# Two PSUM banks shared by the two halves of a convolution and the two sweeps of a second product, with every round in a new order

## The chip, the cores and the metric

The kernel runs on one core of a Trainium2 chip. A core has a matrix engine (PE, with its weight loads shown as PEld), a vector engine (DVE), a scalar engine (ACT), a general engine (POOL) and a queue engine (SP). Each engine works through its own list of instructions in order; semaphores tie the lists together. Matrix products land in PSUM, a memory of eight banks that PE, ACT and DVE can reach. The metric is the device time of one execution in microseconds (us).

## The reference

A causal convolution with seven taps, softmax-normalised per head, and behind it a dense layer with a rational activation:

```
w   = softmax(weight)                                  # 8 heads x 7 taps
xc[b,s,h,:] = sum_k w[h,k] * x[b, s-6+k, h, :]         # 8 x 4096 tokens, 192 features
h   = xc @ w_in                                        # 32768 x 2048
P   = a0 + a1*h + a2*h^2 + a3*h^3
Q   = 1 + |b0|*|h| + |b1|*h^2
out = (P / (Q + 1e-6)) @ w_out                         # 32768 x 192
```

All of it is float32. The convolved `xc`, the hidden `h` and the activation never leave the core.

## The kernel before

The 32768 tokens are cut into 64 **chunks** of 512 (`NCH`). The 2048 hidden features are cut into 8 **units** of 256 for each chunk. A chunk passes through three stages.

- **Convolution** (`conv_part`, L301): PE multiplies band matrices of taps. Half 0 (features of the first 128 rows, 36 matmuls) and half 1 (the other 64 rows, for both halves of the tokens, 18 matmuls) each fill one PSUM bank. A float32 matmul leaves two records in the trace, so the halves show as 72 and 36. ACT copies half 0 out, rounded (`xh`, L310), and DVE takes the remainder (`xl`, L319); half 1 is copied by two pieces on ACT (L313) and two on DVE (L324).
- **First product and activation** of a unit (`gemm1`, L336, 10 matmuls into a two-bank tile `hp`, of which there are two). ACT makes `hs` (a copy, L381), `A` (L401) and `B` (L404); POOL makes `t` in two steps, `p` (L387) and `u` (L394), and starts a DMA that adds `B` to `A` (`Q`, L407); DVE finishes the numerator, `v` (L398); ACT takes logarithm and exponential for the reciprocal, `L` (L410) and `Y` (L413, into a PSUM tile of which there is one); DVE makes `m`, `e`, `g` (L417, L422, L426). The last of `hs`, `A`, `B`, `v` of a unit lets PE write the first product of the unit after next into the same `hp`.
- **Second product** (`gemm2`, L353): for one chunk two **sweeps**, `g20` to `g23` for tokens 0 to 255 and `g24` to `g27` for tokens 256 to 511. Each sweep has 16 **quarters** (a to d) of two matmuls, four records each, and sums in one bank over all 16 blocks of features. `out_evac` (L360, ACT) then copies the bank to `ob`, and SP stores it: `O0` for the first sweep, `O1` for the second.

The order is written by hand in three strings: `START` for the first three rounds, `PLAN`, used for each of the rounds 3 to 62, and `END`. A token such as `g13b.1` names a step, its unit, a piece, and how many chunks back it works. In round i PE runs the convolution of chunk i, the first products mostly of chunk i-1 and the second product of chunk i-2. Each engine sees only its own tokens, in the order of the string; `tc.manual_schedule` keeps it for PE, ACT, DVE and POOL.

Two PSUM banks matter for the change. `ps_c` holds one tile, `cps`, and takes both halves of the convolution, one after the other. `ps_o` holds one tile, `op`, and takes both sweeps of the second product, one after the other; only the very last chunk has its first sweep in `ps_c`. The weights are rounded in START, and their steps (`wi..`, `wo..`) use the same two tiles.

Of the kernel before, what the change touches and what calls it, by code (L numbers as in the profile page):

```python
# [39 lines left out]


PLAN = """
c0.0 O1.2 Q1.1 hs2.1 v1.1 Y7.2 p2.1 g20a.1 B2.1 m7.2 g20b.1 u2.1 g13a.1 A2.1 e7.2 L0.1 g13b.1 g7.2 xh0.0
g20c.1 hs3.1 v2.1 g20d.1 Y0.1 g21a.1 p3.1 g21b.1 A3.1 m0.1 g14a.1 Q2.1 B3.1 e0.1 u3.1 g14b.1 L1.1 g0.1
g21c.1 hs4.1 g21d.1 Q3.1 Y1.1 v3.1 g22a.1 g22b.1 B4.1 p4.1 m1.1 g22c.1 A4.1 g15a.1 u4.1 e1.1 L2.1 g15b.1
g1.1 g22d.1 hs5.1 Q4.1 v4.1 g23a.1 Y2.1 g23b.1 p5.1 xl0.0 g23c.1 B5.1 m2.1 g23d.1 u5.1 L3.1 g16a.1 e2.1
O0.1 A5.1 g16b.1 g2.1 Q5.1 g24a.1 hs6.1 v5.1 g24b.1 Y3.1 g24c.1 p6.1 c1.0 A6.1 m3.1 u6.1 g17a.1 L4.1
e3.1 xh1.0 g17b.1 B6.1 g3.1 g24d.1 hs7.1 g25a.1 xl1.0 g25b.1 Y4.1 p7.1 v6.1 g25c.1 A7.1 g25d.1 m4.1 Q6.1
L5.1 g10a.0 u7.1 e4.1 B7.1 g10b.0 g4.1 g26a.1 hs0.0 Q7.1 g26b.1 v7.1 Y5.1 g26c.1 p0.0 g26d.1 B0.0 m5.1
g11a.0 u0.0 A0.0 e5.1 g11b.0 L6.1 g5.1 g27a.1 hs1.0 Q0.0 g27b.1 v0.0 Y6.1 g27c.1 p1.0 g27d.1 L7.1 m6.1  # L50
g12a.0 u1.0 B1.0 e6.1 g12b.0 A1.0 g6.1
"""


# [2 lines left out]


START = """
wia0.0 c0.0 cf0.0 wid0.0 wis0.0 wid1.0 wio0.0 cf1.0 wia1.0 wir0.0 c1.0 wis1.0 xh0.0 wih0.0 wio1.0 xl0.0  # L60
wia2.0 wir1.0 wid2.0 wip0.0 wis2.0 wih1.0 wio2.0 xh1.0 wil0.0 wir2.0 wia3.0 xl1.0 wip1.0 wid3.0 wis3.0
wid4.0 g10a.0 wio3.0 wih2.0 wil1.0 wia4.0 wir3.0 wid5.0 g10b.0 wis4.0 wih3.0 wio4.0 cf2.0 wir4.0 wip2.0
hs0.0 g11a.0 wia5.0 p0.0 wil2.0 A0.0 wis5.0 u0.0 wio5.0 g11b.0 wih4.0 B0.0 wia6.0 wip3.0 hs1.0 wis6.0
Q0.0 wil3.0 wid6.0 p1.0 B1.0 wio6.0 wip4.0 v0.0 wia7.0 wir5.0 A1.0 wis7.0 g12a.0 u1.0 wih5.0 wio7.0
wod0.0 wil4.0 woa0.0 g12b.0 wid7.0 wos0.0 L0.0 woo0.0 Q1.0 v1.0 woa1.0 wir6.0 Y0.0 wos1.0 g13a.0 woo1.0
hs2.0 wir7.0 m0.0 woa2.0 wip5.0 p2.0 wih6.0 e0.0 A2.0 g13b.0 u2.0 g0.0 B2.0 L1.0 wos2.0 wil5.0 hs3.0
Q2.0 v2.0 wip6.0 Y1.0 p3.0 woo2.0 g14a.0 wod1.0 m1.0 B3.0 wor0.0 g14b.0 wod2.0 e1.0 u3.0 wih7.0 woa3.0
wil6.0 A3.0 wos3.0 wip7.0 hs4.0 woo3.0 Q3.0 v3.0 A4.0 p4.0 g1.0 woa4.0 g15a.0 L2.0 wor1.0 wos4.0 Y2.0
woo4.0 g15b.0 u4.0 wil7.0 woa5.0 m2.0 B4.0 c0.1 hs5.0 wos5.0 Q4.0 v4.0 wod3.0 p5.0 L3.0 e2.0 g16a.0
xh0.1 u5.0 B5.0 g2.0 g16b.0 A5.0 xl0.1 Y3.0 woo5.0 Q5.0 c1.1 v5.0 hs6.0 wor3.0 B6.0 m3.0 g17a.0 p6.0  # L70
xh1.1 e3.0 woa6.0 wor2.0 g17b.0 A6.0 wos6.0 u6.0 L4.0 g3.0 hs7.0 woo6.0 xl1.1 Y4.0 Q6.0 v6.0 wod4.0 p7.0
A7.0 m4.0 g10a.1 B7.0 wor4.0 e4.0 g10b.1 woa7.0 u7.0 L5.0 g4.0 hs0.1 wos7.0 Y5.0 p0.1 woo7.0 v7.0 g20a.1
A0.1 Q7.0 g20b.1 L6.0 m5.0 g11a.1 u0.1 wod6.0 e5.0 B0.1 g11b.1 wod5.0 g20c.1 g5.0 hs1.1 Q0.1 g20d.1 v0.1
g21a.1 Y6.0 p1.1 g21b.1 A1.1 m6.0 g12a.1 wor5.0 B1.1 u1.1 e6.0 g12b.1 L7.0 g6.0 g21c.1 hs2.1 c0.2 Q1.1
v1.1 Y7.0 p2.1 g21d.1 A2.1 m7.0 g13a.1 L0.1 u2.1 e7.0 g13b.1 xh0.2 B2.1 g7.0 g22a.1 hs3.1 Q2.1 g22b.1
xl0.2 Y0.1 g22c.1 v2.1 p3.1 c1.2 wod7.0 L1.1 m0.1 g22d.1 wor6.0 g14a.1 xh1.2 u3.1 e0.1 A3.1 g14b.1 g0.1
B3.1 g23a.1 hs4.1 wor7.0 xl1.2 g23b.1 Y1.1 v3.1 Q3.1 g23c.1 g23d.1 B4.1 p4.1 m1.1 g15a.1 L2.1 u4.1 e1.1
g15b.1 O0.1 A4.1 g24a.1 g1.1 hs5.1 g24b.1 Q4.1 v4.1 g24c.1 Y2.1 p5.1 B5.1 m2.1 g16a.1 A5.1 u5.1 e2.1
g16b.1 L3.1 g24d.1 g2.1 hs6.1 g25a.1 Q5.1 v5.1 g25b.1 Y3.1 g25c.1 p6.1 B6.1 m3.1 g17a.1 L4.1 u6.1 e3.1
g17b.1 A6.1 g3.1 g25d.1 hs7.1 g26a.1 Q6.1 v6.1 Y4.1 g26b.1 p7.1 g26c.1 B7.1 m4.1 g10a.2 u7.1 A7.1 e4.1  # L80
g10b.2 L5.1 g4.1 g26d.1 hs0.2 Q7.1 g27a.1 v7.1 Y5.1 g27b.1 p0.2 g27c.1 A0.2 m5.1 g11a.2 u0.2 B0.2 e5.1
g11b.2 L6.1 g5.1 g27d.1 hs1.2 Q0.2 v0.2 Y6.1 p1.2 L7.1 m6.1 g12a.2 u1.2 B1.2 e6.1 g12b.2 A1.2 g6.1
"""


END = """
c0.1 O1.3 Q1.2 hs2.2 v1.2 Y7.3 p2.2 g20a.2 g20b.2 L0.2 m7.3 u2.2 g13a.2 B2.2 e7.3 g13b.2 A2.2 g7.3
g20c.2 Q2.2 hs3.2 g20d.2 v2.2 xh0.1 g21a.2 p3.2 Y0.2 g21b.2 g21c.2 B3.2 u3.2 m0.2 g14a.2 A3.2 e0.2
g14b.2 L1.2 Q3.2 g0.2 g21d.2 hs4.2 g22a.2 v3.2 Y1.2 g22b.2 p4.2 g22c.2 xl0.1 L2.2 g15a.2 u4.2 m1.2 B4.2
g15b.2 e1.2 A4.2 g22d.2 g1.2 hs5.2 c1.1 p5.2 v4.2 g23a.2 xh1.1 g23b.2 Y2.2 Q4.2 g23c.2 L3.2 g23d.2 m2.2  # L90
u5.2 g16a.2 B5.2 e2.2 O0.2 g16b.2 A5.2 g2.2 g24a.2 Q5.2 hs6.2 v5.2 g24b.2 Y3.2 g24c.2 p6.2 xl1.1 g24d.2
L4.2 g17a.2 u6.2 m3.2 B6.2 g17b.2 e3.2 g25a.2 hs7.2 g3.2 g25b.2 A6.2 g25c.2 p7.2 v6.2 g25d.2 Y4.2 g26a.2
u7.2 B7.2 m4.2 g10a.1 A7.2 e4.2 g10b.1 L5.2 Q6.2 g26b.2 g4.2 hs0.1 g26c.2 v7.2 g26d.2 p0.1 Y5.2 g27a.2
B0.1 m5.2 g27b.2 Q7.2 g27c.2 e5.2 u0.1 g27d.2 g11a.1 O1.2 g5.2 A0.1 g20a.1 L6.2 v0.1 Q0.1 g11b.1 Y6.2
g20b.1 hs1.1 m6.2 g20c.1 g12a.1 A1.1 p1.1 e6.2 L7.2 g12b.1 u1.1 g6.2 B1.1 g20d.1 hs2.1 g21a.1 g21b.1
Y7.2 p2.1 v1.1 g21c.1 B2.1 g21d.1 Q1.1 m7.2 g22a.1 A2.1 g13a.1 u2.1 e7.2 L0.1 g13b.1 g7.2 g22b.1 Q2.1
hs3.1 v2.1 g22c.1 Y0.1 g22d.1 p3.1 g23a.1 A3.1 m0.1 g23b.1 u3.1 L1.1 g23c.1 e0.1 g23d.1 B3.1 g14a.1 g0.1
O0.1 Q3.1 g14b.1 v3.1 Y1.1 g20a.0 L2.1 m1.1 g24a.1 B4.1 g24b.1 e1.1 g15a.1 hs4.1 g1.1 A4.1 p4.1 g24c.1
g24d.1 Y2.1 Q4.1 g15b.1 L3.1 m2.1 u4.1 g25a.1 A5.1 g25b.1 e2.1 B5.1 g20b.0 g25c.1 g2.1 hs5.1 g25d.1 v4.1
g26a.1 p5.1 Y3.1 g26b.1 L4.1 m3.1 Q5.1 g26c.1 g26d.1 e3.1 u5.1 g16a.1 g3.1 g27a.1 g16b.1 v5.1 Y4.1  # L100
g27b.1 A6.1 m4.1 g27c.1 B6.1 g27d.1 e4.1 g20c.0 hs6.1 Q6.1 g17a.1 g4.1 O1.1 p6.1 L5.1 g20d.0 Y5.1 g21a.0
u6.1 g17b.1 m5.1 g24a.0 A7.1 e5.1 g21b.0 B7.1 g21c.0 g5.1 g21d.0 hs7.1 Q7.1 g22a.0 v6.1 L6.1 g24b.0 p7.1
g24c.0 Y6.1 g24d.0 u7.1 m6.1 g22b.0 g25a.0 e6.1 g25b.0 g22c.0 g6.1 g25c.0 L7.1 g25d.0 v7.1 Y7.1 g26a.0
g26b.0 m7.1 g22d.0 g26c.0 e7.1 g23a.0 g7.1 g26d.0 g23b.0 g27a.0 g27b.0 g23c.0 g23d.0 g27c.0 O0.0 g27d.0
O1.0
"""


# [5 lines left out]
def kernel(  # L114
# [52 lines left out]
    def load_x(c):  # L167
        t = xs_buf[c % 2]
        nc.sync.dma_start(out=t[0:BLK, 0:3 * XF // 4], in_=xa[c])
        nc.sync.dma_start(out=t[BLK:, 3 * XF // 4:], in_=xb[c])  # L170
# [165 lines left out]
            nc.tensor.matmul(H[k][:, j, :], lhsT=w[:, i, part, j, :], rhs=x, start=(n == 0), stop=(n == len(terms) - 1))  # L336
# [4 lines left out]

    def gemm2(c, u, q):
        pair, r = divmod(u, 4)
        f = 4 * r + q
# [4 lines left out]
        op = O[c, pair]
        g = G[c * UPC + f // 2]  # L350
        for t in range(2):
            tok = (2 * pair + t) * P
            nc.tensor.matmul(op[:, t, 0:D], lhsT=g[:, f % 2, tok:tok + P], rhs=wo_t[:, f, :],  # L353
                             start=(f == 0 and t == 0), stop=(f == FT - 1 and t == 1))
# [60 lines left out]
    def step_m(k):  # L415
        G[k] = gpool.tile([P, 2, CH], F32, name="g")
        nc.vector.scalar_tensor_tensor(out=G[k].rearrange("p a b -> p (a b)"), in0=st[k]["t"], scalar=a0,  # L417
                                       in1=st[k]["y"], op0=ALU.add, op1=ALU.mult)
# [5 lines left out]
    def step_g(k):  # L424
        g = G[k].rearrange("p a b -> p (a b)")
        nc.vector.scalar_tensor_tensor(out=g, in0=st[k]["y"], scalar=2.0, in1=g, op0=ALU.subtract, op1=ALU.mult)  # L426
# [107 lines left out]
```

## Time and profile before

| what | value |
|---|---|
| time, median of 3 runs (range) | 2715.94 us (2715.7 to 2717.48) |
| profiled execution, its own time | 2716.26 us |
| its span, first to last instruction | 2714.5 us |
| busy ACT / DVE / POOL | 94% / 95% / 85% of the span |
| start of the convolution of chunk 3 (first PLAN round) | 119.59 us |
| start of the convolution of chunk 63 (END) | 2615.53 us |
| granted PE clock, mean | 0.997 |

The span is 1.76 us short of the execution's own time. A row of the timeline gives start, duration, engine, line and operands, and in brackets the idle time before it and who ended it; neighbouring rows of one form are merged with a count. The chain of waits inside a window, in order of time, gives the pieces of work that follow each other on the path that ended last: start, length, engine, tile, line and how many instructions. There the end of each piece is the start of the next, so lengths can be added. A row of the windows view gives the stretch and its length, then how long PE, PEld, DVE, ACT and POOL were busy in it (with instruction counts), the granted PE clock, the share of DMA time and GB/s.

### The profile page before, as it was taken

Reading aid. Unit: us, or ns where it says so; the run is one execution under the profiler, and the core shown is the slowest. Engines: PE = TensorE matmul, PEld = TensorE weight load, DVE = VectorE, ACT = ScalarE, POOL = GpSimd, SP = SyncE. Lnnn points to the kernel's source line nnn. Section 1 sums busy time; section 2 is a strip of 40 time slices with the busy share of each in tenths; the row PEclk is TensorE's granted clock in tenths of the full one; section 3 lists DMA queues with packets and bytes.
Section 4 is the critical chain, followed back from the end, with each engine's and each line's share of the span. In section 5 each row is a group of like instructions: output and inputs, shape, how many; then the busy total and the mean of one; then the engine's idle time right before and its main releaser. Section 6 shows DMA issues by size and latency. Waiting matters only on the chain.

```text
span 2714.5 us, 51342 instructions
## 1 busy us (share of the span) xinstructions
PE 2680.2 (99%) x20248; PEld 2414.1 (89%) x20248; DVE 2587.1 (95%) x2293; ACT 2560.7 (94%) x2927; POOL 2302.7 (85%) x1567
## 2 busy tenths in 40 slices
...
GB/s 192 114 123 126 117 123 121 123 124 119 125 122 120 125 121 117 129 119 126 119 122 124 126 117 123 120 123 124 121 125 120 123 124 120 117 129 119 126 102 93
DMA packets 122786, 332.79 MB, mean 123 GB/s; under 512 B 12848, under 2 KB 51888, under 8 KB 122544
## 3 DMA queue, kind: packets, MB, share of 16 engines
...
q10 hardware_dynamic: 432, 0.20, 0.0%
...
## 4 chain that ended last, share of the span: by engine, by line
PE 94%; DVE 2%; POOL 1%; ACT 1%; issue 1%; DMA 0%; ACTq 0%; POOLq 0%; DVEq 0%
PE op L353 47%; PE hp L336 42%; PE cps L301 4%; POOL t L394 1%; DVE t L398 0%; DVE y L422 0%; PE cps L353 0%; POOL t L387 0%; DMA A<-B 0%; ACT y L413 0%; ACT hs L381 0%; DVE g L426 0%; ACT A L401 0%; DMA wb_t<-in_wband 0%; PE cps L278 0%
## 5 line engine op out<-in xcount | busy, mean ns | idle before, releaser
L353 PE MATMUL op<-wo_t,g 128*128 128x192 f32 x8128 | 1411.4, 327 | 0.6 <-DVE wo_t L268 0.6
L353 PEld LDWEIGHTS op<-wo_t,g 128*128 128x128 f32 x8128 | 1341.6, 190 | 41.7 <-POOL t L394 1.3
L394 POOL TENSOR_TENSOR t<-t,hs 128x1024 f32<-128x1024 f32 x512 | 1268.0, 2476 | 31.6
L387 POOL TENSOR_SCALAR t<-hs,cf 128x1024 f32<-128x1024 f32 x512 | 647.5, 1265 | 290.4 <-ACT hs L381 283.2
L336 PE MATMUL hp<-xh,wh_t 128*128 128x512 f32 x2048 | 871.1, 425 | 12.6 <-DVE t L398 12.6
L417 DVE SCALAR_TENSOR_TENSOR g<-t,cf,y 128x1024 f32<-128x1024 f32 x512 | 655.0, 1279 | 80.4 <-ACT y L413 64.6
L398 DVE SCALAR_TENSOR_TENSOR t<-t,cf,hp 128x1024 f32<-128x1024 f32 x512 | 652.1, 1274 | 6.1 <-POOL t L394 2.8
L426 DVE SCALAR_TENSOR_TENSOR g<-y,g 128x1024 f32<-128x1024 f32 x512 | 627.0, 1225 | 17.5
L336 PE MATMUL hp<-xh,wl_t 128*128 128x512 f32 x2048 | 635.7, 391 | 0.0
L381 ACT COPY hs<-hp 128x1024 f32<-128x1024 f32 x512 | 524.5, 1024 | 117.7 <-PE hp L336 104.8
L422 DVE SCALAR_TENSOR_TENSOR y<-A,y 128x1024 f32<-128x1024 f32 x512 | 625.7, 1222 | 0.0
L410 ACT ACTIVATE B<-A 128x1024 f32<-128x1024 f32 x512 | 551.1, 1076 | 4.5 <-DMA A<-B 4.4
L413 ACT ACTIVATE y<-B 128x1024 f32<-128x1024 f32 x512 | 536.8, 1048 | 10.1 <-DVE g L426 4.4
L407 POOL DMA_DIRECT2D A<-B x512 | 480.2, 938 | 66.6 <-ACT A L401 51.6
L401 ACT ACTIVATE A<-hp 128x1024 f32<-128x1024 f32 x512 | 532.9, 1041 | 1.0 <-PE hp L336 0.9
L404 ACT ACTIVATE B<-hp 128x1024 f32<-128x1024 f32 x512 | 529.8, 1035 | 1.5
L336 PEld LDWEIGHTS hp<-xh,wl_t 128*128 128x128 f32 x2048 | 385.3, 188 | 88.9
L336 PEld LDWEIGHTS hp<-xh,wh_t 128*128 128x128 f32 x2048 | 386.3, 189 | 86.8 <-issue 11.5
L336 PE MATMUL hp<-xl,wh_t 128*128 128x512 f32 x1024 | 404.0, 394 | 0.0
L336 PEld LDWEIGHTS hp<-xl,wh_t 128*128 128x128 f32 x1024 | 193.9, 189 | 20.4
L301 PEld LDWEIGHTS cps<-wb_t,xs 128*32 128x32 f32 x6876 | 120.8, 150 | 45.5 <-issue 43.0
L301 PE MATMUL cps<-wb_t,xs 128*32 128x58 f32 x6876 | 137.1, 228 | 9.0 <-DVE cf L230 7.8
...
## 6 DMA issues: line engine op xcount, KB each, us to landing
A<-B POOLq DMA_DIRECT2D x512, 512.0 KB, 4.6
out<-ob SPq DMA_DIRECT2D x128, 192.0 KB, 1.9
...
```

The costliest lines, as they stand in the source:

```text
L336: nc.tensor.matmul(H[k][:, j, :], lhsT=w[:, i, part, j, :], rhs=x, start=(n == 0), stop=(n == len(terms) - 1))
L353: nc.tensor.matmul(op[:, t, 0:D], lhsT=g[:, f % 2, tok:tok + P], rhs=wo_t[:, f, :], start=(f == 0 and t == 0), stop=(f == FT - 1 and t == 1))
L387: nc.gpsimd.tensor_scalar(tile_of(k, "t", work), st[k]["hs"], a3, a2, ALU.mult, ALU.add)
L394: nc.gpsimd.tensor_tensor(out=t, in0=t, in1=st[k]["hs"], op=ALU.mult)
L398: nc.vector.scalar_tensor_tensor(out=t, in0=t, scalar=a1, in1=flat(k), op0=ALU.add, op1=ALU.mult)
L401: nc.scalar.activation(out=tile_of(k, "A", work), in_=flat(k), func=AF.Abs, scale=scales[0])
L404: nc.scalar.activation(out=tile_of(k, "B", work), in_=flat(k), func=AF.Square, scale=scales[1])
L410: nc.scalar.activation(out=st[k]["B"], in_=st[k]["A"], func=AF.Ln, bias=C_Q)
L413: nc.scalar.activation(out=tile_of(k, "y", ps_y), in_=st[k]["B"], func=AF.Exp, scale=-1.0)
L417: nc.vector.scalar_tensor_tensor(out=G[k].rearrange("p a b -> p (a b)"), in0=st[k]["t"], scalar=a0, in1=st[k]["y"], op0=ALU.add, op1=ALU.mult)
L422: nc.vector.scalar_tensor_tensor(out=y, in0=st[k]["A"], scalar=C_Q, in1=y, op0=ALU.add, op1=ALU.mult)
L426: nc.vector.scalar_tensor_tensor(out=g, in0=st[k]["y"], scalar=2.0, in1=g, op0=ALU.subtract, op1=ALU.mult)
```

## The change

The sweeps and the halves are dealt to the banks anew, from chunk 1 on for the sweeps and from chunk 3 on for the halves:

```diff
     def gemm2(c, u, q):
...
-        if f == 0 and c == NCH - 1 and pair == 0:
+        if f == 0 and pair == 0 and c >= 1:
             O[c, pair] = ps_c.tile([P, 2, 256], F32, name="cps")
         elif f == 0:
             O[c, pair] = ps_o.tile([P, 2, 256], F32, name="op")
...
         if (c, half) == (0, 1):
             CP[c, half] = ps_y.tile([P, W], F32, name="y")[:, 0:CH]
+        elif half == 1 and c >= 3:
+            CP[c, half] = ps_o.tile([P, 2, 256], F32, name="op").rearrange("p a b -> p (a b)")
         else:
             CP[c, half] = ps_c.tile([P, 2, 256], F32, name="cps").rearrange("p a b -> p (a b)")
```

So `ps_c` now goes from half 0 of a convolution to the first sweep and back, and `ps_o` from half 1 to the second sweep and back. The three strings are new throughout; the instructions themselves and their sizes are the same. The first two lines of `PLAN`, before and now:

```diff
 PLAN = """
-c0.0 O1.2 Q1.1 hs2.1 v1.1 Y7.2 p2.1 g20a.1 B2.1 m7.2 g20b.1 u2.1 g13a.1 A2.1 e7.2 L0.1 g13b.1 g7.2 xh0.0
-g20c.1 hs3.1 v2.1 g20d.1 Y0.1 g21a.1 p3.1 g21b.1 A3.1 m0.1 g14a.1 Q2.1 B3.1 e0.1 u3.1 g14b.1 L1.1 g0.1
+c0.0 u1.1 O1.2 B1.1 e6.2 c1.0 L7.2 g6.2 g12a.1 xh0.0 A1.1 xl0.0 g12b.1 Y7.2 Q1.1 v1.1 g20a.1 hs2.1
+g20b.1 m7.2 xh1.0 g13a.1 p2.1 A2.1 e7.2 g13b.1 u2.1 L0.1 g7.2 g20c.1 B2.1 g20d.1 xl1.0 hs3.1 g21a.1 Q2.1
...
```

In a round PE used to run half 0, 2 quarters, `g13`, 4 quarters, `g14`, 5, `g15`, 5, `g16`, 3 and half 1, `g17`, 5, `g10`, 4, `g11`, 4, `g12`. Now it runs both halves, `g12`, 2 quarters, `g13`, 5, `g14`, 4, `g15`, 5, `g16`, 4, `g17`, 4, `g10`, 4, `g11`, 4. From `g24a` to `g22d` the quarters of the two sweeps now alternate irregularly.

PE before, at half 0 of a convolution. The columns are place, line, operation, output and inputs, size and count (here matmuls, not records); `hp` is written by first products, `cps` by the convolution and `op` by the second product:

```order
2744 L336 MATMUL hp<-xh_11010,wl_t 128x512
2745 L301 MATMUL cps<-wb_t,xs_102 32x58 x32
2746 L301 MATMUL cps<-wb_t,xs_102 32x48 x4
2747 L353 MATMUL op<-wo_t,g 128x192 x4
2748 L336 MATMUL hp<-xh_10841,wh_t 128x512
```

Half 0 stands between a first product and the two opening quarters of the first sweep. Half 1 of the same convolution stands four first products later in the round:

```order
2791 L353 MATMUL op<-wo_t,g 128x192 x6
2792 L301 MATMUL cps<-wb_t,xs_102 32x58 x14
2793 L301 MATMUL cps<-wb_t,xs_102 32x48 x2
2794 L301 MATMUL cps<-wb_t,xs_102 32x58 x2
2795 L336 MATMUL hp<-xh_10841,wh_t 128x512
```

It has quarters ahead and a first product behind. PE now, at the one place where a round has its convolution:

```order
2797 L355 MATMUL op<-wo_t,g 128x192 x8
2798 L301 MATMUL cps<-wb_t,xs_102 32x58 x32
2799 L301 MATMUL cps<-wb_t,xs_102 32x48 x4
2800 L301 MATMUL op<-wb_t,xs_102 32x58 x14
2801 L301 MATMUL op<-wb_t,xs_102 32x48 x2
2802 L301 MATMUL op<-wb_t,xs_102 32x58 x2
2803 L336 MATMUL hp<-xh_10077,wh_t 128x512
```

The last quarters of the second sweep (`g27a` to `g27d`) stand ahead, both halves follow each other, and the first product `g12` stands behind. Half 1 writes the bank `op` that those quarters have just filled, so `O1` has to empty it in between.

ACT before, around the same `O1` (`ob<-op`), with the copy of half 0 behind it:

```order
1541 L360 COPY ob<-op 128x384
1542 L381 COPY hs<-hp 128x1024
1543 L413 ACTIVATE y<-B 128x1024
1544 L404 ACTIVATE B<-hp 128x1024
1545 L401 ACTIVATE A<-hp 128x1024
1546 L410 ACTIVATE B<-A 128x1024
1547 L310 CAST xh_12696<-cps 128x512
```

ACT now, from `O1` on (`O1 B1 L7 xh0 A1 Y7 hs2`, the two pieces of `xh1`, `A2 L0 B2`; the next two rows are `hs3` and `Y0`):

```order
1538 L362 COPY ob<-op 128x384
1539 L406 ACTIVATE B<-hp 128x1024
1540 L412 ACTIVATE B<-A 128x1024
1541 L310 CAST xh_12674<-cps 128x512
1542 L403 ACTIVATE A<-hp 128x1024
1543 L415 ACTIVATE y<-B 128x1024
1544 L383 COPY hs<-hp 128x1024
1545 L313 CAST xh_12698<-op 64x290
1546 L313 CAST xh_12698<-op 64x222
1547 L403 ACTIVATE A<-hp 128x1024
1548 L412 ACTIVATE B<-A 128x1024
1549 L406 ACTIVATE B<-hp 128x1024
```

Before, PE went from the last quarters (`g27d`) to a whole first product (`g12`) and half 0, and `O1` could empty the bank meanwhile. Now the last quarters are the last thing that PE does ahead of the convolution, and both copies of the convolution stand close behind `O1` on ACT. On DVE each unit still has `v m e g`; `xl0` now stands ahead of `v1` and `xl1` ahead of `v2`.

START now ends ahead of `g12` of its last round, and END begins with that `g12` behind the convolution of chunk 63.

More of the change, by code (lines that the diff above doesn't have):

```diff
@@ L42 @@
 PLAN = """
-c0.0 O1.2 Q1.1 hs2.1 v1.1 Y7.2 p2.1 g20a.1 B2.1 m7.2 g20b.1 u2.1 g13a.1 A2.1 e7.2 L0.1 g13b.1 g7.2 xh0.0
-g20c.1 hs3.1 v2.1 g20d.1 Y0.1 g21a.1 p3.1 g21b.1 A3.1 m0.1 g14a.1 Q2.1 B3.1 e0.1 u3.1 g14b.1 L1.1 g0.1
[L45 to L51, printed above, removed]
+c0.0 u1.1 O1.2 B1.1 e6.2 c1.0 L7.2 g6.2 g12a.1 xh0.0 A1.1 xl0.0 g12b.1 Y7.2 Q1.1 v1.1 g20a.1 hs2.1
+g20b.1 m7.2 xh1.0 g13a.1 p2.1 A2.1 e7.2 g13b.1 u2.1 L0.1 g7.2 g20c.1 B2.1 g20d.1 xl1.0 hs3.1 g21a.1 Q2.1
+v2.1 g21b.1 Y0.1 p3.1 g24a.1 L1.1 m0.1 g14a.1 u3.1 B3.1 e0.1 g14b.1 A3.1 g0.1 g24b.1 hs4.1 Q3.1 g21c.1
+v3.1 Y1.1 g24c.1 p4.1 g21d.1 A4.1 m1.1 g15a.1 u4.1 B4.1 e1.1 g15b.1 L2.1 g1.1 g22a.1 hs5.1 Q4.1 g24d.1
+v4.1 Y2.1 g25a.1 p5.1 g22b.1 A5.1 m2.1 g25b.1 u5.1 L3.1 g16a.1 e2.1 B5.1 g16b.1 g2.1 Q5.1 g25c.1 hs6.1
+v5.1 g22c.1 Y3.1 g25d.1 p6.1 g22d.1 A6.1 m3.1 g17a.1 u6.1 L4.1 e3.1 g17b.1 B6.1 g3.1 g23a.1 Q6.1 hs7.1
+g23b.1 v6.1 Y4.1 g23c.1 p7.1 g23d.1 B7.1 m4.1 g10a.0 u7.1 A7.1 e4.1 g10b.0 L5.1 g4.1 g26a.1 Q7.1 hs0.0
+g26b.1 v7.1 Y5.1 g26c.1 p0.0 g26d.1 A0.0 m5.1 g11a.0 u0.0 B0.0 e5.1 g11b.0 L6.1 g5.1 g27a.1 O0.1 Q0.0
+hs1.0 g27b.1 v0.0 g27c.1 Y6.1 p1.0 g27d.1 m6.1
 """
@@ L59 @@
 START = """
[L60 to L79, printed above, removed]
@@ L80 @@
-g17b.1 A6.1 g3.1 g25d.1 hs7.1 g26a.1 Q6.1 v6.1 Y4.1 g26b.1 p7.1 g26c.1 B7.1 m4.1 g10a.2 u7.1 A7.1 e4.1
-g10b.2 L5.1 g4.1 g26d.1 hs0.2 Q7.1 g27a.1 v7.1 Y5.1 g27b.1 p0.2 g27c.1 A0.2 m5.1 g11a.2 u0.2 B0.2 e5.1
-g11b.2 L6.1 g5.1 g27d.1 hs1.2 Q0.2 v0.2 Y6.1 p1.2 L7.1 m6.1 g12a.2 u1.2 B1.2 e6.1 g12b.2 A1.2 g6.1
+wia0.0 c0.0 wid0.0 wis0.0 cf0.0 wid1.0 wio0.0 cf1.0 wia1.0 wir0.0 c1.0 wis1.0 xh0.0 wih0.0 wio1.0 xl0.0
+wia2.0 wir1.0 cf2.0 wip0.0 wis2.0 wid2.0 wio2.0 xh1.0 wil0.0 wir2.0 wih1.0 wia3.0 xl1.0 wip1.0 wid3.0
@@ new lines @@
+wis3.0 wid4.0 g10a.0 wio3.0 wid5.0 wil1.0 wir3.0 wia4.0 g10b.0 wih2.0 wis4.0 wid6.0 wio4.0 wih3.0 wip2.0
+wir4.0 hs0.0 g11a.0 wia5.0 p0.0 wil2.0 A0.0 wis5.0 u0.0 wio5.0 g11b.0 wih4.0 B0.0 wia6.0 wip3.0 hs1.0
+wis6.0 Q0.0 wio6.0 B1.0 p1.0 wil3.0 wia7.0 v0.0 wip4.0 wid7.0 wir5.0 A1.0 wis7.0 g12a.0 u1.0 wih5.0
+wio7.0 wil4.0 woa0.0 g12b.0 wos0.0 L0.0 woo0.0 Q1.0 v1.0 wip5.0 woa1.0 hs2.0 wir6.0 wos1.0 g13a.0 Y0.0
+wil5.0 p2.0 woo1.0 B2.0 m0.0 g13b.0 u2.0 woa2.0 wih6.0 e0.0 A2.0 wip6.0 g0.0 hs3.0 Q2.0 L1.0 v2.0 p3.0
@@ new lines @@
+Y1.0 wos2.0 g14a.0 wir7.0 woo2.0 wod1.0 wil6.0 A3.0 u3.0 m1.0 g14b.0 wod0.0 B3.0 e1.0 wih7.0 hs4.0
+wor0.0 g1.0 wip7.0 woa3.0 wor1.0 v3.0 L2.0 p4.0 Y2.0 wos3.0 g15a.0 wil7.0 Q3.0 wod4.0 m2.0 B4.0 g15b.0
+u4.0 A4.0 woo3.0 e2.0 wod3.0 c0.1 woa4.0 hs5.0 Q4.0 wos4.0 v4.0 B5.0 p5.0 A5.0 woo4.0 g16a.0 g2.0 u5.0
+woa5.0 xh0.1 wos5.0 g16b.0 L3.0 xl0.1 Y3.0 woo5.0 wor4.0 c1.1 v5.0 hs6.0 Q5.0 m3.0 g17a.0 L4.0 p6.0 A6.0
+e3.0 wor3.0 g17b.0 xh1.1 g3.0 u6.0 woa6.0 B6.0 xl1.1 hs7.0 wos6.0 woo6.0 Q6.0 Y4.0 v6.0 A7.0 p7.0 m4.0
@@ new lines @@
+g10a.1 B7.0 u7.0 wod2.0 e4.0 g10b.1 L5.0 c0.2 g4.0 wod7.0 hs0.1 Q7.0 v7.0 woa7.0 p0.1 Y5.0 wos7.0 g11a.1
+woo7.0 wor2.0 B0.1 m5.0 g11b.1 A0.1 u0.1 e5.0 wod5.0 g20a.1 hs1.1 g20b.1 g5.0 g20c.1 L6.0 wor5.0 g20d.1
+v0.1 Y6.0 p1.1 L7.0 m6.0 g12a.1 Q0.1 A1.1 e6.0 g21a.1 u1.1 B1.1 g12b.1 g6.0 xh0.2 g21b.1 hs2.1 xl0.2
+Q1.1 g21c.1 Y7.0 v1.1 g21d.1 p2.1 wod6.0 m7.0 g13a.1 A2.1 u2.1 B2.1 e7.0 g13b.1 L0.1 g22a.1 g7.0 wor6.0
+hs3.1 g22b.1 v2.1 g22c.1 Q2.1 Y0.1 g22d.1 B3.1 p3.1 m0.1 g14a.1 A3.1 u3.1 g14b.1 e0.1 L1.1 g23a.1 g0.1
@@ new lines @@
+hs4.1 c1.2 wor7.0 v3.1 Y1.1 g23b.1 Q3.1 g23c.1 L2.1 m1.1 g23d.1 p4.1 A4.1 g15a.1 e1.1 B4.1 u4.1 g15b.1
+g1.1 xh1.2 O0.1 xl1.2 hs5.1 g24a.1 Q4.1 v4.1 g24b.1 Y2.1 g24c.1 p5.1 B5.1 m2.1 g16a.1 L3.1 u5.1 e2.1
+g16b.1 A5.1 g24d.1 g2.1 hs6.1 g25a.1 Q5.1 v5.1 g25b.1 Y3.1 p6.1 B6.1 m3.1 g17a.1 L4.1 u6.1 e3.1 g17b.1
+A6.1 g25c.1 g3.1 hs7.1 g25d.1 Q6.1 v6.1 g26a.1 Y4.1 p7.1 L5.1 m4.1 g10a.2 u7.1 A7.1 e4.1 g10b.2 B7.1
+g26b.1 g4.1 hs0.2 g26c.1 Q7.1 v7.1 g26d.1 Y5.1 p0.2 g27a.1 A0.2 m5.1 g11a.2 u0.2 L6.1 e5.1 g11b.2 B0.2
@@ L83 @@
+g5.1 g27b.1 hs1.2 g27c.1 v0.2 Y6.1 g27d.1 p1.2 m6.1 Q0.2
 """
 END = """
[L87 to L105, printed above, removed]
+c0.1 u1.2 O1.3 L7.3 e6.3 c1.1 xh0.1 B1.2 g12a.2 xl0.1 v1.2 xh1.1 g12b.2 A1.2 g6.3 g20a.2 hs2.2 g13a.2
+xl1.1 Y7.3 p2.2 g20b.2 L0.2 m7.3 g24a.2 Q1.2 g13b.2 A2.2 e7.3 u2.2 B2.2 g24b.2 g7.3 g24c.2 hs3.2 g24d.2
```

17 lines of the change are left out of this document (added).

## The prediction

> **What bounds the kernel now.** The page's first section gives PE a full bar. The chain of waits in one round, from the convolution of one chunk to that of the next, shows what the bar is made of.
>
> ```profile
> PE 2680.2 (99%) x20248; PEld 2414.1 (89%) x20248; DVE 2587.1 (95%) x2293; ACT 2560.7 (94%) x2927; POOL 2302.7 (85%) x1567
> ```
>
> ```profile
> 1201.43 1.25 PE cps L301 x71
> 1202.68 1.50 PE op L353 x8
> 1204.17 2.28 PE hp L336 x10
> 1206.45 2.60 PE op L353 x16
> 1209.05 2.28 PE hp L336 x10
> 1211.33 3.25 PE op L353 x20
> 1214.58 2.32 PE hp L336 x10
> ...
> 1222.47 1.95 PE op L353 x12
> 1224.42 0.75 PE cps L301 x34
> 1225.17 2.50 PE hp L336 x10
> ...
> 1242.99 1.02 PE cps L301 x56
> ```
>
> A round is 1242.99 - 1201.43 = 41.56 us, and no engine but PE is in its chain. The windows view, over the 60 PLAN rounds, START's second half and END, says the same: in the rounds PE is busy for all but 0.78 us, while DVE has 2400.42 / 60 = 40.0 us of work in a round and ACT 39.6.
>
> ```profile
> 60.00:119.59 59.59, 52.83 (x351) 44.29 (x350) 57.90 (x55) 58.07 (x68) 55.92 (x40) 0.97 0.58 120
> 119.59:2615.53 2495.94, 2495.16 (x18961) 2255.80 (x18960) 2400.42 (x2101) 2377.20 (x2702) 2137.26 (x1441) 1.00 0.59 122
> 2615.53:2711.00 95.47, 95.00 (x623) 88.61 (x622) 82.08 (x70) 75.44 (x86) 63.32 (x44) 1.00 0.45 94
> ```
>
> So the rounds and END are PE's own work. A shorter time needs less of PE's time in a round, and PE's gain counts only until ACT or DVE make it wait. START is different: PE has 6.8 us idle there and DVE 1.7.
>
> **What a convolution costs PE.** A second-product record takes 3.25 / 20 = 0.1625 us. The 8 behind half 0 would be 1.30, and took 1.50: half 0 costs 1.25 + 0.20 = 1.45. A first product takes 2.28, the one behind half 1 took 2.50: half 1 costs 0.75 + 0.22 = 0.97. Together 2.42 us a round, in which each half pays its own way into and out of other work.
>
> Now both halves are one run of 108 records. From above it costs 1.25 + 0.75 = 2.00 (nothing saved at the seam). From below, 36 more records cost 1.25 - 0.75 = 0.50 each time, so 0.75 + 2 x 0.50 = 1.75. I take the middle, 1.87, since nothing favours an end. Behind it stands a first product: 2.50.
>
> The new round: the run 1.87; eight first products, of which one at 2.50, two behind 20 records at 2.32 (three before) and five at 2.28, together 18.54; 128 second-product records at 0.1625, 20.80. **Sum 41.21, 0.35 less** (0.22 to 0.47 by the two ends).
>
> The alternating sweeps I cost at nothing. END of before alternates already, and changes bank after each quarter at the same 0.65 / 4 = 0.1625 us:
>
> ```profile
> 2704.35 0.65 PE op L353 x4
> 2705.00 0.65 PE cps L353 x4
> ```
>
> One page of the Trainium skill speaks against such an order. "TensorE: Matmul & The Clock Gate", section "A second HAM failure mode: psum-queue depth-cycling", tells of a kernel that cycled through PSUM banks, whose matrix engine paused so often between groups that its clock gate kept swinging. By that rule the alternating stretch would run below the full clock; by this trace, where END alternates at a granted clock of 1.00, it does not.
>
> **The wait that is added.** Half 1 now writes the bank that `g27d` has just filled, so ACT's `O1` cannot start before PE ends its last quarter. What is queued behind `O1` on ACT is thereby tied to PE. I follow it with ACT's rows, which give starts one after another:
>
> ```profile
> 2653.16 0.48 ACT L360 COPY ob<-op 128x384 f32<-128x384 f32 x1 [1.61 <-PE op L353]
> 2653.53 1.03 ACT L401 ACTIVATE A<-hp 128x1024 f32<-128x1024 f32 x1
> ```
>
> ```profile
> 1205.29 1.11 ACT L410 ACTIVATE B<-A 128x1024 f32<-128x1024 f32 x1
> 1206.24 0.63 ACT L310 CAST xh<-cps 128x512 fp32r<-128x512 f32 x1
> 1206.70 1.08 ACT L381 COPY hs<-hp 128x1024 f32<-128x1024 f32 x1
> 1207.60 1.11 ACT L413 ACTIVATE y<-B 128x1024 f32<-128x1024 f32 x1
> 1208.56 1.10 ACT L401 ACTIVATE A<-hp 128x1024 f32<-128x1024 f32 x1
> 1209.47 1.10 ACT L404 ACTIVATE B<-hp 128x1024 f32<-128x1024 f32 x1
> 1210.37 1.15 ACT L410 ACTIVATE B<-A 128x1024 f32<-128x1024 f32 x1
> 1211.43 1.01 ACT L381 COPY hs<-hp 128x1024 f32<-128x1024 f32 x1
> 1212.53 1.03 ACT L413 ACTIVATE y<-B 128x1024 f32<-128x1024 f32 x1
> ...
> 1226.28 0.74 ACT L313 CAST xh<-cps 64x290 fp32r<-64x290 f32 x2
> 1227.04 1.03 ACT L404 ACTIVATE B<-hp 128x1024 f32<-128x1024 f32 x1
> ```
>
> From start to next start: `O` 0.37; `L` to `xh0` 0.95; `xh0` 0.46; `hs` 0.90; `Y` 0.96; `A` 0.91; `B` 0.90; `xh1` 0.76. ACT's new order is O1 0.37, B1 0.90, L7 0.95, xh0 0.46, A1 0.91, Y7 0.96, hs2 0.90, xh1 0.76, A2 0.91, L0 0.95, B2 0.90, hs3 0.90, then Y0: **9.87 us from O1 to Y0**. Three of these pairs (`A` to `Y`, `L` to `B`, `B` to `hs`) have no quoted row; the nearest above is `L` to `hs`, 1.06, so 0.42 more at worst, and 0.90 from below. DVE goes on from Y0:
>
> ```profile
> 1213.59 1.28 DVE L417 SCALAR_TENSOR_TENSOR g<-t,cf,y 128x1024 f32<-128x1024 f32 x1
> 1214.79 1.22 DVE L422 SCALAR_TENSOR_TENSOR y<-A,y 128x1024 f32<-128x1024 f32 x1
> 1216.04 1.22 DVE L426 SCALAR_TENSOR_TENSOR g<-y,g 128x1024 f32<-128x1024 f32 x1
> 1217.18 1.27 DVE L398 SCALAR_TENSOR_TENSOR t<-t,cf,hp 128x1024 f32<-128x1024 f32 x1
> ```
>
> `m` starts 1213.59 - 1212.53 = 1.06 behind Y's start, and `v` 3.59 behind `m`. `v3` frees the tile `hp` that `g15` needs. What PE does with a late `v` is seen once in END:
>
> ```profile
> 2644.59 1.29 DVE t L398
> 2645.89 0.14 issue
> 2646.02 2.55 PE hp L336 x10
> 2648.57 4.55 PE op L353 x28
> ```
>
> The first product ends 2648.57 - 2645.88 = 2.69 behind the end of `v`. The last quarter there ends at 2648.57 + 4.55 = 2653.12, and `O` starts at 2653.16, 0.04 later.
>
> Count from the end of `g27d`. By way of ACT and DVE, `g15` ends at 0.04 + 9.87 + 1.06 + 3.59 + 1.28 + 2.69 = 18.53. By PE's own work it ends at 1.87 + 2.50 + 1.30 + 2.28 + 3.25 + 2.32 + 2.60 + 2.28 = 18.40. So PE waits 0.13 us at `g15`, in every round, since the next `O1` is tied to PE again: **round 41.34, 0.22 less than 41.56**.
>
> Half 1 itself does not wait: `O1` is over at 0.04 + 0.48 = 0.52, and half 0 keeps PE for at least 1.0. `xh0` ends at 2.26 + 0.63 = 2.89 and `xl0` takes under a microsecond of DVE more, well before `g20a` at 4.37.
>
> **START and END.** The cut between START and PLAN moves ahead of `g12`, and ahead of the steps `e` and `g` of one unit (1.25 + 1.14 = 2.39 us of DVE by the rows above). START is held by DVE and ACT (57.90 and 58.07 of 59.59), so it ends some 2.4 earlier; END is PE's and takes the 2.28 of that first product, less 0.35 for its own convolution. Net -0.5. The new order inside START I take as equal. It could win the 1.7 that DVE idles and lose about half of what PE idles, 3.4.
>
> Sum, against the profiled execution's own 2716.26 (0.3 over the median of the runs): 60 x 0.22 = 13.2 and 0.5 off, **2702.6**.
>
> **The rivals.**
>
> No wait. If ACT's run is 0.13 shorter than I add up (0.011 a step), PE never waits: 60 x 0.35 + 0.5 off, 2694.8. For it: END and the rounds of before keep PE waiting for nothing. Chance 0.22.
>
> The seam saves nothing. The run costs 2.00 as two halves did; PE's round is 41.34, and `g15` is then reached 0.13 later too, so it does not wait. That is 2702.6 again, by another road. With a second way in paid at the seam (0.20), the round is 41.54 and the time about 2714.5. Chance 0.06 for the latter, since both halves use the same taps and the same input.
>
> ACT's wide steps are 0.95 apart throughout, as behind L410. Nine of them then cost 8.55, not 8.28; PE waits 0.40, the round is 41.61 and the time about 2719, no change. For it: DVE and ACT have under 2 us of slack in a round of 41.2. Chance 0.14. "ScalarE: Activation LUTs" of the Trainium skill, section "What ACT_TABLE_LOAD costs", gives 186 ns + 0.833 ns an element, with 93 ns of overlap, hence an estimated 0.946 us for 1024 elements; this trace has 0.90 for `hs` and `B`, and the measurement decides.
>
> Slower. The three pairs without a row all cost 1.06: ACT's run is 10.29, PE waits 0.55 at `g15`, the round is 41.76, and the time 2716.3 + 60 x 0.20 - 0.5 = 2728. It decides from a wait of 0.44 on (60 x 0.09 = 5.4 us, about 0.2%, is the least that a measurement here tells from no change). Chance 0.10.
>
> The clock falls where the sweeps alternate (16 us of a round, `g24a` to `g22d`). At START's mean clock of 0.97 that is 0.5 us a round, about 2733. Against it stands END. Chance 0.01.
>
> **How the numbers follow.** The likeliest, PE waits 0.05 to 0.25 at `g15`, has 0.47: 2702.6, with 2698 to 2710 as its own range. With START's -1.7 the no-wait case reaches down to 2693. To leave out no more than 2 in 10, the range also takes in the paid seam: **2693 to 2715**. Faster by over 0.2% (under 2710.8): the likeliest and no wait, and a part of the paid seam and of the 0.95 steps, 0.74. Within 0.2%: the rest of these, 0.15. Slower: 0.11.
>
> **What would show it.** In the changed profile's chain of a round: the convolution as one piece of about 1.87 with 2.50 behind it; a wait of PE for DVE's L398 (now L400) of about 0.1 at the first product that follows the four mixed quarters, some 16 us behind the convolution, and none elsewhere; `ob<-op` on ACT waiting for PE in every round. The step on the seam is wrong if the run is at 1.75 or 2.0. The step on ACT is wrong if the wait is absent or stands at another first product (`g13` or `g14`), or if POOL ends it. The whole is wrong if rounds are longer than 41.56 without PE waiting, or if the convolution of chunk 3 starts later than 120 us.

## The result and the profile after

| kernel | time, median (range) | ratio to before (95% interval) |
|---|---|---|
| before | 2715.94 us (2715.33 to 2718.0, 5 runs) | |
| after | 2702.71 us (2701.7 to 2704.53, 5 runs) | 0.9950 (0.9939 to 0.9961) |

The change makes the kernel 13.2 us faster, 0.5%. The profiled execution of after took 2701.7 us, its span is 2700.0.

The first section of the page of after: PE is as full as before, with 11.6 us less to do, and the instructions are as many.

```profile
PE 2668.6 (99%) x20248; PEld 2410.6 (89%) x20248; DVE 2593.8 (96%) x2293; ACT 2568.7 (95%) x2927; POOL 2311.3 (86%) x1567
```

The windows view of after, over the second half of START, the 60 PLAN rounds and END:

```profile
60.00:115.55 55.55, 49.30 (x337) 42.23 (x337) 53.83 (x51) 54.50 (x64) 51.34 (x36) 0.97 0.57 116
115.55:2598.93 2483.38, 2482.33 (x18961) 2251.24 (x18960) 2407.38 (x2102) 2384.95 (x2701) 2147.53 (x1442) 1.00 0.59 123
2598.93:2698.00 99.07, 96.99 (x633) 90.41 (x632) 84.57 (x72) 78.38 (x88) 65.55 (x45) 1.00 0.46 97
```

The convolution of chunk 3 starts 4.04 us earlier (119.59 to 115.55). The 60 rounds take 2483.38 instead of 2495.94, 12.56 less. From 2598.93 to the end of the span is 101.07, where it was 98.97: 2.1 more, as the spans are given to 0.1. Together that is 14.5, the whole difference of the spans (2714.5 and 2700.0). The granted clock in the rounds is 1.00, as before.

The chain of waits through the first part of one round of after, in order of time (start, length, engine, tile, line, records). The round runs from 1316.4 to 1357.8, 41.3 us:

```profile
1316.44 1.26 PE cps L301 x71
1317.70 0.59 PE op L301 x32
1318.29 2.50 PE hp L336 x10
1320.79 1.30 PE cps L355 x8
1322.09 2.28 PE hp L336 x10
1324.37 2.60 PE cps L355 x16
1326.97 0.65 PE op L355 x4
1327.62 2.41 PE hp L336 x10
1330.03 0.65 PE op L355 x4
1330.68 0.65 PE cps L355 x4
1331.33 0.65 PE op L355 x4
1331.98 0.65 PE cps L355 x4
1332.63 2.34 PE hp L336 x10
```

Three things stand there. Both halves are one run of 1.26 + 0.59 = 1.85 us with a first product of 2.50 behind, where the two halves of before had cost 1.45 and 0.97 beyond the ordinary work. The quarters keep their 0.65, alternating or not. And two first products are a little long: `g14`, the third behind the convolution, has 2.41 where the trace of before had 2.32 behind 20 records, and `g15` 2.34 where the others have 2.28. That is taken to be PE waiting, 0.09 and 0.06 us. Over 59 rounds (starts of the piece ahead, of the first product and of the next piece) the medians say the same: `g14` costs 0.09 more than where nothing is late, `g15` 0.05, and the two together 0.15 of a round of 41.34 (each a median of its own). Without these, PE's own round is 41.19. The view of waits does not show them as such: it lists only 11 on `v`, one of PE and 10 of its weight loads. What speaks for waits is that `g14` ends 2.62 behind the end of `v2` and `g15` 2.62 behind the end of `v3`, by the median of the 59 rounds.

```profile
PEld hp L336 <- DVE t L400: 3.2, 10, 1.1
```

The same view (125 to 2590 us) has a wait of the bank's copy for PE once in each round of the window (us in total, times, longest):

```profile
ACT ob L362 <- PE op L355: 26.9, 59, 0.5
```

ACT in another round of after, whose convolution starts at 1275.04 (start, length, engine, line, operation, output and inputs, idle before):

```profile
1275.15 0.48 ACT L362 COPY ob<-op 128x384 f32<-128x384 f32 x1 [0.47 <-PE op L355]
1275.53 1.04 ACT L406 ACTIVATE B<-hp 128x1024 f32<-128x1024 f32 x1
1276.45 1.06 ACT L412 ACTIVATE B<-A 128x1024 f32<-128x1024 f32 x1
1277.39 0.58 ACT L310 CAST xh<-cps 128x512 fp32r<-128x512 f32 x1
1277.86 1.05 ACT L403 ACTIVATE A<-hp 128x1024 f32<-128x1024 f32 x1
1278.77 1.05 ACT L415 ACTIVATE y<-B 128x1024 f32<-128x1024 f32 x1
...
1285.07 1.05 ACT L415 ACTIVATE y<-B 128x1024 f32<-128x1024 f32 x1
```

From `O1` to `Y0` is 1285.07 - 1275.15 = 9.92 us; the prediction had 9.87. DVE in the same round:

```profile
1278.31 0.68 DVE L319 TENSOR_TENSOR xl<-cps,xh 128x512 fp32r<-128x512 f32 x1
1279.02 1.28 DVE L400 SCALAR_TENSOR_TENSOR t<-t,cf,hp 128x1024 f32<-128x1024 f32 x1
...
1282.66 1.22 DVE L428 SCALAR_TENSOR_TENSOR g<-y,g 128x1024 f32<-128x1024 f32 x1
...
1284.81 1.28 DVE L400 SCALAR_TENSOR_TENSOR t<-t,cf,hp 128x1024 f32<-128x1024 f32 x1
1286.15 1.28 DVE L419 SCALAR_TENSOR_TENSOR g<-t,cf,y 128x1024 f32<-128x1024 f32 x1
...
1289.75 1.27 DVE L400 SCALAR_TENSOR_TENSOR t<-t,cf,hp 128x1024 f32<-128x1024 f32 x1
```

The last three are `v2`, `m0` and `v3`, the arm that the prediction follows: `m0` stands 1.08 behind `Y0`, `v3` 3.60 behind `m0`. The first `v` is `v1`. It starts 0.11 behind the end of `A1` on ACT (1277.86 + 1.05 = 1278.91), and `A1` stands behind `O1` as well. So there may be a second arm from `O1`, by `A1`, `v1`, the `m e g` of unit 7 of the chunk before, `xl1` and `v2`, and `v2` frees the `hp` of `g14`. The prediction had not followed that one; whether it is what delays `g14` is for the experiments. That `v1` waits for `A1` the trace itself tells: both read the same `hp`, and in each of the 59 rounds `v1` carries a wait for the semaphore that `A1` raises and starts 0.11 or more behind its end.

### The profile page after: what moved, and what is told of

It is laid out like the page before. It is cut to its first block, busy times and chain, and to the rows that moved or that the text cites. A ratio compares the mean times of both kernels' runs of the same rounds, so it can differ in the third digit from the quotient of the medians.

```text
span 2700.0 us, 51206 instructions
## 1 busy us (share of the span) xinstructions
PE 2668.6 (99%) x20248; PEld 2410.6 (89%) x20248; DVE 2593.8 (96%) x2293; ACT 2568.7 (95%) x2927; POOL 2311.3 (86%) x1567
## 4 chain that ended last, share of the span: by engine, by line
PE 94%; ACT 2%; DVE 2%; issue 1%; POOL 1%; DMA 0%; ACTq 0%; POOLq 0%; DVEq 0%
PE hp L336 42%; PE op L355 24%; PE cps L355 24%; PE cps L301 3%; PE op L301 1%; DVE t L400 1%; POOL t L396 1%; DVE y L424 0%; ACT hs L383 0%; POOL t L389 0%; ACT B L406 0%; ACT y L415 0%; ACT B L412 0%; ACT A L403 0%; DMA A<-B 0%
## 5 line engine op out<-in xcount | busy, mean ns | idle before, releaser
L396 POOL TENSOR_TENSOR t<-t,hs 128x1024 f32<-128x1024 f32 x512 | 1236.7, 2416 | 41.6
L389 POOL TENSOR_SCALAR t<-hs,cf 128x1024 f32<-128x1024 f32 x512 | 641.0, 1252 | 175.5 <-ACT hs L383 166.7
L355 PE MATMUL op<-wo_t,g 128*128 128x192 f32 x4160 | 770.1, 326 | 0.2 <-ACT ob L362 0.2
L355 PE MATMUL cps<-wo_t,g 128*128 128x192 f32 x4032 | 747.9, 326 | 0.1
L355 PEld LDWEIGHTS op<-wo_t,g 128*128 128x128 f32 x4160 | 697.6, 190 | 21.7 <-ACT ob L362 0.6
L355 PEld LDWEIGHTS cps<-wo_t,g 128*128 128x128 f32 x4032 | 676.1, 190 | 20.5 <-DVE xl L319 1.0
L409 POOL DMA_DIRECT2D A<-B x512 | 450.6, 880 | 146.4 <-DVE xl L319 84.0
L412 ACT ACTIVATE B<-A 128x1024 f32<-128x1024 f32 x512 | 543.6, 1062 | 2.7 <-DMA A<-B 2.7
L403 ACT ACTIVATE A<-hp 128x1024 f32<-128x1024 f32 x512 | 525.0, 1025 | 2.3 <-DVE t L400 0.8
```

Of the source, the lines that this page charges most:

```text
L389: nc.gpsimd.tensor_scalar(tile_of(k, "t", work), st[k]["hs"], a3, a2, ALU.mult, ALU.add)
L396: nc.gpsimd.tensor_tensor(out=t, in0=t, in1=st[k]["hs"], op=ALU.mult)
L403: nc.scalar.activation(out=tile_of(k, "A", work), in_=flat(k), func=AF.Abs, scale=scales[0])
L412: nc.scalar.activation(out=st[k]["B"], in_=st[k]["A"], func=AF.Ln, bias=C_Q)
```

## The experiments

The theory: the gain is the seam alone, by way of PE's own round; `O1`, tied to the end of PE's last quarter, takes 0.15 of it back through ACT and DVE. The rivals: the two waits hang on something else (the single bank of `Y`, the first sweep's copy `O0`, POOL); or the gain comes from the rest of the new order and not from the seam. All kernels are after with one edit to the order. Their times, and the ratio to the kernel before:

| kernel | time, median (range) | ratio (95% interval) | median round |
|---|---|---|---|
| `x1_b1_ahead_of_o1` | 2695.79 (2695.0 to 2697.26) | 0.9925 (0.9910 to 0.9941) | 41.20 |
| `x2_o0_earlier` | 2702.82 (2702.17 to 2704.37) | 0.9952 (0.9937 to 0.9967) | 41.34 |
| `x3_both_moves` | 2695.49 (2694.75 to 2696.05) | 0.9923 (0.9910 to 0.9937) | 41.23 |
| `x4_halves_apart` | 2716.89 (2716.43 to 2718.05) | 1.0002 (0.9993 to 1.0011) | 41.59 |
| `x5_old_start` | 2703.21 (2701.81 to 2704.16) | 0.9952 (0.9936 to 0.9969) | 41.34 |
| `x6_a1_before_l7` | 2712.53 (2711.8 to 2713.98) | 0.9984 (0.9974 to 0.9993) | 41.51 |

### A step ahead of the copy that waits

`B1` needs only its first product, not the bank. Put ahead of `O1`, it fills the 0.47 us in which ACT idles there, and what stands behind comes earlier by up to that much.

```diff
-c0.0 u1.1 O1.2 B1.1 e6.2 c1.0 L7.2
+c0.0 u1.1 B1.1 O1.2 e6.2 c1.0 L7.2
```

> The changed kernel with one step moved in each PLAN round: on ACT the step B1 stands ahead of O1 instead of behind it, so that the run which is tied to the last quarter of PE is one step shorter. Theory (ACT's run from O1 to Y0 sets the round of 41.34 us; DVE's run from m6 to v2 is almost as long and only shares the wait): Y0 comes 0.4 us earlier, the wait at g15 (0.06 us) goes, the wait at g14 (0.10) stays because DVE sets it, round 41.29, time about 2699.5. Rival 1 (DVE's run alone sets the round): round 41.34 and time 2702.7 unchanged. Rival 2 (PE's own work is 41.34 and the long first products are no waits): unchanged too, here and in the next two runs. Half 1 may wait up to 0.1 us for O1, which now ends about when half 0 does.

Measured: 2695.79, 6.9 us below after. The chain of a round of this kernel has both waits gone:

```profile
1326.14 2.32 PE hp L336 x10
...
1331.06 2.28 PE hp L336 x10
```

These are `g14` and `g15`, at the lengths of 2.32 behind 20 records and 2.28 elsewhere. ACT of the same round, in which the last quarter ends and the convolution's piece of the chain begins at 1314.96:

```profile
1314.41 1.05 ACT L406 ACTIVATE B<-hp 128x1024 f32<-128x1024 f32 x1
1315.32 0.52 ACT L362 COPY ob<-op 128x384 f32<-128x384 f32 x1
```

`O1` now starts 0.36 behind the end of the last quarter instead of 0.04 and waits for nothing, with `B1` all but over. Half 1 does not have to wait for it as a rule: the convolution is 1.86 on average over the rounds, 2.035 at most. The round is shorter by 0.14, nearly the whole 0.15. I had expected a part of `g14`'s wait to stay; it went, which speaks for the arm by `A1`, since in this kernel `A1` comes 0.6 earlier too (2.21 behind the convolution by the median, 2.81 in after). `Y0` came only 0.16 earlier (9.86 behind the convolution), not the 0.4 that I had expected: `Y7` now starts 0.09 behind the end of `g6` on DVE, which frees its PSUM tile. The room is small. `g14` and `g15` end 2.65 behind `v2` and `v3` here, and 2.62 where they wait.

The rivals on `Y` and `O0` did not expect this; `O0` was not moved, and `Y6`, which stands two steps behind it, keeps its place (1.41 ahead of the next convolution, 1.43 in after), and yet both waits are gone.

### The first sweep's copy, earlier

```diff
-g11a.0 u0.0 B0.0 e5.1 g11b.0 L6.1 g5.1 g27a.1 O0.1 Q0.0
+g11a.0 u0.0 O0.1 B0.0 e5.1 g11b.0 L6.1 g5.1 g27a.1 Q0.0
```

> The changed kernel with one step moved in each PLAN round: on ACT the step O0 stands ahead of B0 instead of between L6 and hs1, so that hs1 and Y6, and with Y6 the run m6 to v2 on DVE, start 0.15 to 0.2 us earlier; O1 is tied to PE as before. Theory (ACT's run from O1 sets the round): the wait at g14 goes, the one at g15 grows from 0.06 to 0.15, round 41.34 and time 2702.7 unchanged. Rival 1 (DVE's run sets the round): both waits shrink, round 41.2 to 41.25, time 2694 to 2697. Rival 2 (no waits): unchanged, with the same lengths at g14 and g15 as before the move.

Measured: 2702.82, the same as after, and both waits as they were (2.42 and 2.32 in the chain of one round). But the steps that should have moved, `hs1` and `Y6` on ACT and `m6` on DVE, did not start earlier either (`Y6` at 1.44 ahead of the convolution, 1.43 in after). `O0` came 1.85 earlier, but ACT's run there has no gap, so what stands behind both places ends up where it was. So the edit hardly changed what it was to change, and by itself it says little of the rival.

The trace of after says more of the other two. `Y0` starts 1.18 behind the end of `g7`, which frees the tile of `Y` (1282.66 + 1.22 = 1283.88 and 1285.07 in the rows above), so the single tile does not hold it. POOL's `u` ends 1.45, 0.27 and 0.54 ahead of the start of `v1`, `v2` and `v3`, so POOL does not end their waits (medians of 59 rounds).

### Both

> The changed kernel with both steps moved, B1 ahead of O1 and O0 ahead of B0. Theory and rival 1 both: no wait is left, round 41.19 to 41.22, 0.12 to 0.15 less, time 2693.5 to 2695.5, which beats the changed kernel. Rival 2 (PE's own work is 41.34): unchanged, 2702.7.

Measured: 2695.49, within the error of the first edit alone. With it, this is the fastest version of the study, 0.77% below before.

### The halves apart again

Half 1 (`c1`) behind `g12` instead of ahead of it, all else as in after; the waits for `O1` then have more room too.

```diff
-e6.2 c1.0 L7.2 g6.2 g12a.1 xh0.0 A1.1 xl0.0 g12b.1 Y7.2
+e6.2 L7.2 g6.2 g12a.1 xh0.0 A1.1 xl0.0 g12b.1 c1.0 Y7.2
```

> The changed kernel with half 1 of the convolution moved behind the first product g12 in each PLAN round, so that each half pays its own way in and out again; nothing else moves. Theory (the gain on PE is that the halves follow each other, 2.42 us against 1.86 + 0.22): PE's own round rises by 0.34 to 41.53, the waits at g14 and g15 are covered by it, time about 2714. Rival (the seam is worth nothing, the gain comes from the new order elsewhere): round 41.34, time 2702.7.

Measured: 2716.89, the time of before, with a round 0.06 longer than I had expected. The chain at the convolution of one round:

```profile
700.05 1.26 PE cps L301 x71
701.32 2.49 PE hp L336 x10
703.81 0.76 PE op L301 x35
704.57 1.50 PE cps L355 x8
706.07 2.31 PE hp L336 x10
```

These five pieces take 8.33 us; the same work in after, the first five of its chain above, takes 1324.37 - 1316.44 = 7.93. The seam is worth 0.40 in these rounds, and 0.41 by the medians of all. Here PE waits for nothing in a round (`g14` and `g15` have their usual lengths), and 41.59 - 0.41 is 41.18, the 41.19 that after has without its waits. So of all that the change reorders, only the adjacency of the halves gains anything in the rounds: without it the round is 41.59, and that of before is 41.57.

### The old order inside START

The steps of `START` in the order of before, less the eight (`L7.1`, `g12` and `e6.1 g6.1` among them) that after has moved into the first PLAN round.

```diff
-wia0.0 c0.0 wid0.0 wis0.0 cf0.0 wid1.0 wio0.0 cf1.0 wia1.0 wir0.0 c1.0 wis1.0 xh0.0 wih0.0 wio1.0 xl0.0
...
+wia0.0 c0.0 cf0.0 wid0.0 wis0.0 wid1.0 wio0.0 cf1.0 wia1.0 wir0.0 c1.0 wis1.0 xh0.0 wih0.0 wio1.0 xl0.0
...
```

> The changed kernel with the START order of before, cut where the new one ends (the eight steps that now belong to the first PLAN round are taken out of it). The prediction's sum (the cut alone makes START 2.4 us shorter, the new order inside START is worth nothing): the convolution of chunk 3 starts at 117.2 us and the time is 2704.4, so that 1.65 of the 4.0 us that START became shorter come from its order. Rival (all 4.0 come from the cut): it starts at 115.5 and the time is 2702.7.

Measured: 2703.21, the same as after within the runs' spread. The convolution of chunk 3 starts at 115.12 here, earlier than in the one trace of after (115.55), but the first PLAN round then takes 43.04 instead of 41.87. The order inside START is worth nothing that can be measured.

The other runs show how far a single trace can be trusted there. With the same START, chunk 3 started at 115.55, 116.18, 116.65, 116.96, 117.79 and 117.97 in the six profiled executions. The mean, 116.85, is 2.7 ahead of before's single 119.59.

### The arm by A1

If `v1` waits for `A1`, then `A1` ahead of `L7` takes `g14`'s wait away and leaves `g15`'s, since ACT's whole run up to `Y0` has the same steps.

```diff
-O1.2 B1.1 e6.2 c1.0 L7.2 g6.2 g12a.1 xh0.0 A1.1 xl0.0
+O1.2 B1.1 e6.2 c1.0 A1.1 g6.2 g12a.1 xh0.0 L7.2 xl0.0
```

> The changed kernel with A1 and L7 exchanged on ACT in each PLAN round: O1 B1 A1 xh0 L7 Y7 instead of O1 B1 L7 xh0 A1 Y7. The run from O1 to Y0 keeps its length, but A1, which ends at 3.86 us of the round now and releases v1 on DVE at 3.98, ends 1.4 us earlier. Theory (two arms hang on O1: A1, v1, m7, e7, g7, xl1, v2 to g14, and the rest of ACT's run to Y0, m0, e0, g0, v3 to g15, and the longer one sets the round): v1 starts at 3.86, the wait at g14 falls from 0.10 to about 0.03, the wait at g15 grows from 0.06 to about 0.12, round 41.33 to 41.34, time 2702.5. Rival (the arm through v1 alone sets the round): the waits fall and the second does not grow, round 41.22 to 41.25, time 2695.5 to 2697.5.

Measured: 2712.53, 9.8 us slower than after. `v1` came earlier (3.87 behind the convolution by the median, 3.98 in after), no longer with a wait for ACT of its own, and `g14`'s wait fell from 0.09 to 0.02, as expected. But `g15` got worse. The chain of one round:

```profile
1338.63 0.04 issue
1338.67 2.60 PE hp L336 x10
```

`g15` takes 2.64 with the wait instead of 2.28, and 0.30 too much by the median. ACT shows why:

```profile
1325.24 1.09 ACT L412 ACTIVATE B<-A 128x1024 f32<-128x1024 f32 x1
1326.37 1.03 ACT L415 ACTIVATE y<-B 128x1024 f32<-128x1024 f32 x1
```

`Y7` now stands directly behind `L7`, whose result it reads. It starts 0.04 after `L7` ends, 1.13 behind its start, while two independent steps of this width start some 0.9 to 0.95 apart. That lengthens the run from `O1` to `Y0`, which I had expected to keep its length; `Y0` comes 10.20 behind the convolution by the median, 0.18 later than the 10.02 of after. On DVE `m0` waits for it:

```profile
1333.75 1.28 DVE L419 SCALAR_TENSOR_TENSOR g<-t,cf,y 128x1024 f32<-128x1024 f32 x1 [0.32 <-ACT y L415]
```

The round grew by 0.17, almost the 0.18 that `Y0` was late. The wait at `g15` is the old 0.05, the 0.07 that `g14` no longer takes, and this 0.18: 0.30, as measured. So the edit failed as a way to a faster kernel, and showed the theory twice: taking `A1` off the arm frees `g14`, and what is added between `O1` and `Y0` is added to the round, nearly one for one.

## Why the prediction held, and where it did not

**The seam: right, a little small.** Taken was 0.35 off PE's own round (41.21). It is 41.19, and the seam alone 0.41 by the kernel with the halves apart. The run of 108 records has 1.855 by the median where 1.87 was taken, the first product behind it the 2.50 that was expected. A seam that saves nothing or has its own price is refuted.

**The alternating sweeps: right.** They cost nothing: quarters of 0.65 at a granted clock of 1.00 over all 60 rounds, in the changed kernel too.

**The added wait: right in size, wrong in place.** "PE waits 0.13 at `g15` and none elsewhere" was the step; PE waits 0.15, some 0.05 of it at `g15` and 0.09 at `g14`, one of the places that the prediction itself had named as a sign of being wrong. The arm from `O1` by `Y0` to `v3` was as worked out, and its length by luck in part. ACT's run was 0.04 longer (9.91 us by the median, 9.87 predicted) and `m0` stood 0.03 further behind `Y0` (1.09, 1.06 predicted), while the first product ended 2.62 behind a late `v` and not 2.69, which had been read from a single case in END. These cancel; with 2.69 PE would have waited about 0.22. What failed was to take this arm for the only one: the prediction did not ask what `v1` and `v2` wait for, and who else reads the same `hp` ahead of them. `v1` starts once `A1` on ACT is over, and `A1` stands behind `O1` too. That the total came out nearly the same has a reason: what PE waits at `g14` it need not wait again at `g15`, so the longer arm sets the sum and the other only the place. The kernel with `A1` ahead shows it: what left `g14` turned up at `g15`.

**No wait, as a rival: wrong for this kernel,** but one step away. With `B1` ahead of `O1` the round is 41.20 and the time 2695.8; the rival had 41.21 and 2694.8.

**ACT's steps 0.95 apart, or the unseen pairs at 1.06: wrong here.** The run was 0.04 longer than taken, not 0.27 or 0.42; the three pairs without a row measured 0.92, 0.95 and 0.90. What the rivals said of a longer run is true, though: in the kernel with `A1` ahead it grew by 0.18 and PE waited for it. But the cause there was another one, a step that reads what the one ahead of it has just written (1.13 apart).

**START and END: near, and the last digit is luck.** END took 2.1 more (1.93 predicted). START came 4.04 earlier in this one trace (2.4 predicted), of which the six executions with this START leave 2.7 as a mean. The prediction had all rounds alike. The first PLAN round was 0.53 longer than the median, and all 60 together took 2.99 more than 60 medians, where those of before took 1.92 more; so the rounds gave 12.56, where the medians (41.567 and 41.340) would give 13.6. These deviations cancel, and 2702.6 against 2702.71 is closer than the terms of the sum are. What in START makes one execution differ from the next by up to 2.4 us was not looked into.
